# The first value load of a local-attention and gated-MLP kernel, issued right behind the up-projection weights

## The chip, the cores and the metric

The kernel runs on one core of a Trainium2 chip. The metric is device time in microseconds, the median of several executions. Three executions of the kernel before gave 264.83, 264.84 and 265.99 us, a median of 264.84. One further execution was profiled; all durations below come from it.

## The reference

The input x has 2048 tokens of width 640, in bf16. It is layer-normalised once, and two branches read the result:

```python
xn = _layernorm(x)                       # no gain, no bias
# branch A: 32 heads of width 20, window of 8 taps, 2 tokens apart, looking back
q, k, v = split(xn @ wqkv)
logits = einsum("bhsd,bhswd->bhsw", q, k[idx]) * 20 ** -0.5   # idx = pos - 2*w
logits = where(idx >= 0, logits, -1e9)
o = einsum("bhsw,bhswd->bhsd", softmax(logits), v[idx])
A = o @ wo
# branch B: bilinear gated MLP, hidden width 1536
B = ((xn @ w_gate) * (xn @ w_up)) @ w_down
out = x + A + B
```

Each token thus attends to itself and to the tokens 2, 4, ... 14 places before it, head by head.

## The kernel before, in words

**Tiles and chunks.** The 2048 tokens are 16 tiles of 128 (index t). Four tiles form a chunk of 512 (index c, 0 to 3). For each chunk, TensorE (PE) transposes or SyncE's DMA transposes the normalised tiles to `xnT` (lines 345 and 339), computes q and k (line 405) and, tile by tile, v (line 438). ScalarE (ACT) copies the results out of PSUM. v goes to a scratch tensor `vD` in DRAM (line 459, issued by GpSimd, POOL) with 14 rows of zeros in front, because the attention needs each row of v at eight shifts.

**Logits of a chunk.** VectorE (DVE) multiplies q by k at the eight shifts (line 476, `PW[8c]` to `PW[8c+7]`). Two products share one buffer called `pw`. PE adds them up per head in two groups of 40 matmuls (line 490, `LL[2c]`, `LL[2c+1]`), ACT copies the sums to `L` (line 503), and two DMA transposes on SyncE's queue (line 511, `SS[2c]`, `SS[2c+1]`) turn them to `LT`. These two are the chunk's logit transposes. DVE and ACT make the softmax weights `a` out of `LT` (lines 522 to 544; the first DVE step needs both transposes).

**Values of a tile.** One DMA on SyncE's queue (line 554, step `V8[t]`) gathers eight shifted copies of a tile's rows from `vD` to a buffer `v8`, 1280 KB. DVE multiplies it by the weights (line 579), folds the eight copies (lines 588, 592, 594) to `o`, and a DMA transpose (line 601, `OE[t]`) makes `oT`. The `v8` buffers and the `pw` buffers share one ring of five (`tag="pv"`, `bufs=5`): in chunk 0 the four `pw` buffers come first, `v8` of tile 0 takes the fifth, and `v8` of tile 1 takes over the first `pw` buffer, once `LL[0]` has read it.

**Gate, up, down.** PE computes gate and up for a chunk in 24 groups of five matmuls (line 621), ACT copies them (line 626), DVE multiplies the pair to `hT` (line 637, steps `HT[c, f]`, f from 0 to 11). Then, tile by tile, PE sums the down projection and the output projection in one PSUM tile (lines 662 and 665), DVE adds x (line 672) and a DMA stores the rows. The down projection of a chunk's first tile starts with `hT` 0 to 9.

**The order of the work.** A planner (`Plan.order`) simulates the engines with costs written in the code, and picks on each engine, among the steps that are ready, the one with the earliest latest start. The order that it finds is the order in which the instructions are emitted, and each engine runs its own in that order. What an instruction waits for at run time is only its data: who wrote what it reads, and who still reads what it overwrites. The `after=[...]` arguments, the costs and `floor` (an earliest planned end) act in the planner alone. For a DMA with `kb` set the planner also keeps one line of transfers per issuing engine, at 340 KB a microsecond, behind a start of 2 us.

**SyncE's queue around the change.** In the order of issue: w_gate (`wg`), x of tiles 9 to 12, w_up (`wu`, step `WL["u"]`), then chunk 0's two logit transposes, then `V8[0]`, `V8[1]`, w_down (`wd`), `V8[2]`, the transpose of o of tile 0 (`OE[0]`), four loads of `wo` (line 230), `V8[3]`. The list variable `SPLAST[0]` carries this chain in the planner. For `V8[0]` the planner's conditions are: behind `SPLAST[0]`, behind `PW[6]`, and the first stores of `vD` landed.

Of the kernel before, what the change touches and what calls it, by code (L numbers as in the profile page):

```python
# [31 lines left out]
class Plan:  # L32
# [8 lines left out]
    def add(self, eng, cost, fn, deps=(), occ=None, after=(), kb=0):  # L41
        s = Step(eng, cost, fn, deps, occ, after)
        s.kb = kb
        s.idx = len(self.steps)
        self.steps.append(s)
        return s
# [51 lines left out]
def kernel(  # L98
# [58 lines left out]
    def new(key, shape, dtype, tag, bufs, pool=None):  # L157
        t = (pool or sb).tile(shape, dtype, name=tag, tag=tag, bufs=bufs)
        T[key] = t
        return t  # L160
# [305 lines left out]
    PW, LL, LE, SS, DD, AA, O16, OE, V8, DT = {}, {}, {}, {}, {}, {}, {}, {}, {}, {}  # L466

    def prodlog(c):
        for g in range(2):
            for j in range(4):  # L470
                i = 4 * g + j

                def mul(i=i):
                    if i % 2 == 0:
                        new(("pw", c, i // 2), [P, 2, KT, CS], BF, "pv", 5)
                    nc.vector.tensor_tensor(T["pw", c, i // 2][:, i % 2, :, :], T["q", c][:],  # L476
                                            T["k", c][:, :, DIL * i : DIL * i + CS], ALU.mult)

                m = 8 * c + i
                w = [LL.get(2 * c - 1), O16.get(4 * c - 4), O16.get(4 * c - 3), O16.get(4 * c - 2)][i // 2]  # L480
                PW[m] = add("DVE", 1.48, mul, [*Q[c], *Kk[c], w], occ=1.395, after=[PW.get(m - 1) if i else V8.get(4 * c - 1)])
        LASTPW[c] = PW[m]
        for g in range(2):
            n = 2 * c + g

            def lg(g=g):
                l = new(("lps", c, g), [P, 512], F32, "pl", 2, psum)
                for i in range(KT):
                    for j in range(4):
                        nc.tensor.matmul(l[H * j : H * (j + 1), :], lhsT=Ek[:, i, :], rhs=T["pw", c, 2 * g + j // 2][:, j % 2, i, :],  # L490
                                         start=(i == 0), stop=(i == KT - 1), tile_position=(0, H * j),
                                         skip_group_check=True)

            LL[n] = add("PE", 1.25, lg, [PW[m], LL.get(n - 1), LE.get(n - 2), LE.get(n - 1 - g), CE], occ=1.12)
            LL[n].urgent = True
            LL[n].margin = 0.9

            def ev(g=g):
                L = new(("L", c, g), [P, CS], BF, "L", 2)
                if c == 0:  # L500
                    ps = T["lps", c, g]
                    nc.vector.tensor_tensor(ps[:, 0:HALO], ps[:, 0:HALO], negm[:, g, :], ALU.add)
                nc.scalar.copy(L[:], T["lps", c, g][:])

            LE[n] = add("ACT", 0.585, ev, [LL[n], SS.get(n - 2), CM], occ=0.5)

            def tr(g=g):
                if g == 0:
                    new(("LT", c), [P, CH, W, H], BF, "LT", 1)
                out = T["LT", c][:].rearrange("p t (g w) h -> p t g (w h)", g=2)[:, :, g, :]  # L510
                nc.sync.dma_start_transpose(out=out, in_=T["L", c, g][:])

            early = [SPLAST[0]] if c == 0 else []
            SS[n] = SPLAST[0] = add("SP", 3.5, tr, [LE[n], DD.get(2 * c - 1), DD.get(2 * c - 2)], occ=1.25, after=early, kb=160)

    def softmax(c, hf):
        n = 2 * c + hf

        def mx():
            L4 = T["LT", c][:, 2 * hf : 2 * hf + 2, :, :]  # L520
            m = sb.tile([P, 2, 4, H], BF, name="m", tag="m", bufs=1)
            nc.vector.tensor_tensor(m[:], L4[:, :, 0:4, :], L4[:, :, 4:8, :], ALU.max)
            nc.vector.tensor_tensor(m[:, :, 0:2, :], m[:, :, 0:2, :], m[:, :, 2:4, :], ALU.max)
            nc.vector.tensor_tensor(m[:, :, 0:1, :], m[:, :, 0:1, :], m[:, :, 1:2, :], ALU.max)
            d = new(("d", n), [P, 2, W, H], F32, "d", 2)
            nc.vector.tensor_tensor(d[:], L4, m[:, :, 0:1, :].to_broadcast([P, 2, W, H]), ALU.subtract)

        DD[n] = add("DVE", 1.52, mx, [SS[2 * c], SS[2 * c + 1], AA.get(n - 2)], occ=1.43)

        def ex():  # L530
            nc.scalar.activation(T["d", n][:], T["d", n][:], ACT.Exp, scale=scale)

        e = add("ACT", 0.635, ex, [DD[n]], occ=0.54)
        e.margin = 0.8

        def nrm():
            d = T["d", n]
            s = sb.tile([P, 2, 4, H], F32, name="s", tag="s", bufs=1)
            nc.vector.tensor_tensor(s[:], d[:, :, 0:4, :], d[:, :, 4:8, :], ALU.add)
            nc.vector.tensor_tensor(s[:, :, 0:2, :], s[:, :, 0:2, :], s[:, :, 2:4, :], ALU.add)  # L540
            nc.vector.tensor_tensor(s[:, :, 0:1, :], s[:, :, 0:1, :], s[:, :, 1:2, :], ALU.add)
            nc.vector.reciprocal(s[:, :, 0, :], s[:, :, 0, :])
            a = new(("a", n), [P, 2, W, H], BF, "a", 2)
            nc.vector.tensor_tensor(a[:], d[:], s[:, :, 0:1, :].to_broadcast([P, 2, W, H]), ALU.mult)

        AA[n] = add("DVE", 2.33, nrm, [e, O16.get(2 * n - 3)], occ=2.24)

    def load_v8(t):
        def fn():
            v = new(("v8", t), [P, W, D], BF, "pv", 5)  # L550
            r0 = t * P
            src = vD[r0 : r0 + P, :]
            src = bass.AP(tensor=src.tensor, offset=src.offset, ap=[[D, P], [DIL * D, W], [1, D]])
            nc.sync.dma_start(out=v[:], in_=src)
        order = [SPLAST[0]] if t < CH - 1 else [SS[2 * (t // CH) + 1]] if t % CH in (1, 2) else []
        c, u = divmod(t, CH)
        order.append(V8[t - 1] if u else PW[8 * c + 6])
        if t == 3:
            order.append(WL["o"])
        w = LL[2 * c + (u - 1) // 2] if u else O16.get(t - 1)  # L560
        V8[t] = add("SP", 6.0, fn, [VS[t], VS.get(t - 1), w, CZ], occ=0.5, after=order, kb=1280)
        if t < 3:
            SPLAST[0] = V8[t]
            V8[t].floor = (43.5, 0, 0)[t]

    def load_down():
        WL["d"] = SPLAST[0] = add("SP", 8, wload(wd, B_w_down), after=[SPLAST[0]], occ=0.5, kb=1920)
# [4 lines left out]
    def av(t):  # L572
        n, u = divmod(t, 2)
        if t > 2:
            load_v8(t)

        def mul():
            v = T["v8", t]
            nc.vector.tensor_tensor(  # L579
                v[:].rearrange("p w (j h) -> p w j h", j=Dh, h=H),  # L580
                v[:].rearrange("p w (j h) -> p w j h", j=Dh, h=H),
                T["a", n][:, u, :, None, :].to_broadcast([P, W, Dh, H]),
                ALU.mult,
            )

        def tree():
            v = T["v8", t]
            nc.vector.tensor_tensor(v[:, 0:4, :], v[:, 0:4, :], v[:, 4:8, :], ALU.add)  # L588

        def tree2():  # L590
            v = T["v8", t]
            nc.vector.tensor_tensor(v[:, 0:2, :], v[:, 0:2, :], v[:, 2:4, :], ALU.add)  # L592
            o = new(("o", t), [P, D], BF, "o", 2)
            nc.vector.tensor_tensor(o[:], v[:, 0, :], v[:, 1, :], ALU.add)

        a = add("DVE", 2.82, mul, [AA[n], V8[t]], occ=2.735)
        b = add("DVE", 1.485, tree, [a], occ=1.4)

        def tr():
            o = new(("oT", t), [P, KT, P], BF, "oT", 4)  # L600
            nc.sync.dma_start_transpose(out=o[:], in_=T["o", t][:])

        O16[t] = add("DVE", 1.35, tree2, [b, OE.get(t - 2)], occ=1.26)
        OE[t] = add("SP", 2.8, tr, [O16[t], DT.get(t - 4)], occ=1.3, kb=200, after=[V8[2]])
        if t == 0:
            SPLAST[0] = OE[0]
            load_out()
# [151 lines left out]
    def attention(c):  # L759
        if c == 0:  # L760
            SPLAST[0] = WL["u"]
        prodlog(c)
        if c == 0:
            load_v8(0)
            load_v8(1)
            load_down()
            load_v8(2)
        for hf in range(2):
            softmax(c, hf)
        for q in range(CH):  # L770
            av(c * CH + q)
# [47 lines left out]
```

## Time and profile before

| what | value |
|---|---|
| profiled execution: its time, and its span in the trace | 264.88 us, 263.2 us |
| PE busy, share of the span | 258.5 us, 98% |
| DVE busy | 214.7 us, 82% |
| ACT busy | 106.0 us, 40% |
| the sixteen value loads (1280 KB each), median time from issue to landing | 10.0 us |
| w_up, issue to landing | 12.2 us |
| w_down, issue to landing | 17.7 us |
| chunk 0's logit transposes, each | 2.4 and 2.5 us |

The granted TensorE clock was at full speed in all 40 slices of the span. In the lines below, the first two numbers of a timeline line are its start in the span and its length, and a bracket at the end holds the idle time of that engine just before, with what ended it. A time "to landing" runs from the issue of a DMA to its completion. In lists of waits the three numbers are the sum, how many times, and the longest. SPq is SyncE's own instruction queue, from which its DMAs are issued.

### The profile page before, as it was taken

The page shows a single profiled execution, that of the slowest core. Times are in us where ns is not written, and L with a number is a line of the kernel's source. Part 1 is how long each engine was busy: PE and PEld are TensorE (multiplying, and loading weights), DVE is VectorE, ACT ScalarE, POOL GpSimd, SP SyncE. Part 2 cuts the span into 40 slices and gives each one's busy share as a digit, 9 for nine tenths or more (in the row PEclk, how much of TensorE's full clock was granted, in tenths as well). Part 3 has the DMA queues.
Part 4 walks back from the last instruction along what each step waited for, and adds up shares of the span by engine and source line. Part 5 has one row for each costly group of instructions (what it writes and reads, how often), then busy time and mean ns, then how long its engine had stood idle before and what let it go on. Part 6 is the DMA issues. An engine that isn't in the chain of part 4 may idle for free.

```text
span 263.2 us, 4101 instructions
## 1 busy us (share of the span) xinstructions
PE 258.5 (98%) x1574; PEld 140.9 (54%) x1574; DVE 214.7 (82%) x337; ACT 106.0 (40%) x197; POOL 39.3 (15%) x84
## 2 busy tenths in 40 slices
PE   7999999999999999999999999999999999999995
PEld 2645455444677446444477554644456764445763
DVE  5775997799899999999999189999992999993221
ACT  2755557555200347455510155655541105554000
POOL 4651036000021121400001000420000004000000
PEclk9999999999999999999999999999999999999999
DMA  7998927999989149931167299451903985111001
GB/s 220 334 198 270 399 106 190 381 362 253 287 188 278 50 99 369 310 112 29 25 124 251 66 305 322 99 149 25 199 28 70 364 296 134 28 25 25 27 25 50
DMA packets 50707, 46.55 MB, mean 177 GB/s; under 512 B 24786, under 2 KB 47840, under 8 KB 50688
## 3 DMA queue, kind: packets, MB, share of 16 engines
q1 hardware_dynamic: 46704, 37.10, 50.1%
q0 software_dynamic: 2384, 8.05, 8.9%
q10 hardware_dynamic: 1600, 1.15, 1.4%
q8 instruction: 12, 0.20, 0.3%
q14 instruction: 7, 0.06, 0.1%
HBM read 35.39 MB, written 5.26 MB: 154 GB/s over the span
## 4 chain that ended last, share of the span: by engine, by line
PE 78%; DVE 11%; DMA 7%; SPq 1%; issue 0%; ACT 0%; DVEq 0%
PE ps L621 30%; PE ps L662 15%; PE ps L405 15%; DMA pv<-vD 7%; PE ps L438 7%; PE ps L665 6%; DVE pv L476 4%; DVE pv L579 3%; PE pl L490 3%; PE ps L242 2%; DVE xr L672 1%; DVE pv L588 1%; SPq L230 1%; DVE pv L592 1%; PE ps L345 0%
## 5 line engine op out<-in xcount | busy, mean ns | idle before, releaser
L621 PE MATMUL ps<-xnT,wg 128*128 128x512 bf16 x240 | 59.6, 379 | 0.0
L621 PE MATMUL ps<-xnT,wu 128*128 128x512 bf16 x240 | 59.6, 379 | 0.0
L662 PE MATMUL ps<-wd,hT 128*128 128x320 bf16 (+2 forms) x384 | 57.4, 299 | 0.0
L476 DVE TENSOR_TENSOR pv<-q,k 128x2560 bf16<-128x2560 bf16 x32 | 46.5, 1484 | 3.0 <-ACT k L412 3.0
L579 DVE TENSOR_TENSOR pv<-pv,a 128x5120 bf16<-128x5120 bf16 x16 | 45.1, 2820 | 3.0 <-DMA pv<-vD 2.9
L662 PEld LDWEIGHTS <-hT 128*128 128x128 bf16 x384 | 37.0, 98 | 16.5 <-issue 0.8
L626 ACT CAST gs<-ps 128x512 bf16<-128x512 f32 x48 | 28.2, 587 | 32.2 <-PE ps L621 32.2
L621 PEld LDWEIGHTS <-wu 128*128 128x128 bf16 x240 | 23.5, 98 | 28.3
L621 PEld LDWEIGHTS <-wg 128*128 128x128 bf16 x240 | 23.5, 98 | 27.7
L626 ACT CAST us<-ps 128x512 bf16<-128x512 f32 x48 | 28.2, 587 | 22.4 <-PE ps L621 22.0
L672 DVE TENSOR_TENSOR xr<-ps,xr 128x320 bf16<-128x320 f32 (+2 forms) x32 | 15.0, 486 | 24.5 <-PE ps L665 16.1
L665 PE MATMUL ps<-wo,oT 128*128 128x320 bf16 (+2 forms) x160 | 27.0, 299 | 0.0
L696 POOL DMA_DIRECT2D out_dram<-xr x14 | 7.6, 542 | 125.8 <-DVE xr L672 119.2
L588 DVE TENSOR_TENSOR pv<-pv 128x2560 bf16<-128x2560 bf16 x16 | 23.8, 1485 | 0.1
L438 PE MATMUL ps<-wv,xnT 128*128 128x320 bf16 x160 | 23.3, 300 | 0.4 <-ACT xnT L351 0.4
L412 ACT CAST q<-ps 128x512 bf16<-128x512 f32 x20 | 11.7, 585 | 27.8 <-PE ps L405 27.8
L637 DVE TENSOR_TENSOR hT<-gs,us 128x512 bf16<-128x512 bf16 x48 | 19.5, 419 | 4.0 <-ACT us L626 4.0
L405 PE MATMUL ps<-xnT,wq 128*128 128x512 bf16 x100 | 22.4, 379 | 0.0
L405 PE MATMUL ps<-xnT,wk 128*128 128x512 bf16 x100 | 22.2, 379 | 0.0
L438 PEld LDWEIGHTS <-xnT 128*128 128x128 bf16 x160 | 15.3, 98 | 7.5 <-ACT xnT L351 0.6
L665 PEld LDWEIGHTS <-oT 128*128 128x128 bf16 x160 | 15.5, 98 | 6.3
L444 ACT CAST v_t<-ps 128x320 bf16<-128x320 f32 x32 | 13.3, 429 | 7.4 <-PE ps L438 4.1
(54 smaller groups left out, 178.7 us busy)
## 6 DMA issues: line engine op xcount, KB each, us to landing
pv<-vD SPq DMA_DIRECT2D x16, 1280.0 KB, 10.0
vD<-v_t POOLq DMA_DIRECT2D x16, 160.0 KB, 4.5
xr<-in_A_x_dram POOLq DMA_DIRECT2D x16, 160.0 KB, 3.7
out_dram<-xr POOLq DMA_DIRECT2D x14, 160.0 KB, 3.5
wg<-in_B_w_gate_dram SPq DMA_DIRECT2D x1, 1920.0 KB, 8.1
wu<-in_B_w_up_dram SPq DMA_DIRECT2D x1, 1920.0 KB, 12.2
wd<-in_B_w_down_dram SPq DMA_DIRECT2D x1, 1920.0 KB, 17.7
x<-in_A_x_dram SPq DMA_DIRECT2D x11, 160.0 KB, 4.9
```

The source lines that it names most:

```text
L405: nc.tensor.matmul(T[key][:, 0:n], lhsT=(wk if r else wq)[:, i, j * P : (j + 1) * P], rhs=T["xnT", c][:, i, lo : lo + n], start=(i == 0), ...
L438: nc.tensor.matmul(T["psv", t, n][:, 0:NS], lhsT=T["xnT", c][:, i, q * P : (q + 1) * P], rhs=wv[:, i, n * NS : (n + 1) * NS], start=(i == ...
L444: nc.scalar.copy(T["v_t", t][:].rearrange("p (j h) -> p j h", j=Dh, h=H)[:, :, n * H // 2 : (n + 1) * H // 2], T["psv", t, n][:, 0:NS].rea ...
L476: nc.vector.tensor_tensor(T["pw", c, i // 2][:, i % 2, :, :], T["q", c][:], T["k", c][:, :, DIL * i : DIL * i + CS], ALU.mult)
L579: nc.vector.tensor_tensor(v[:].rearrange("p w (j h) -> p w j h", j=Dh, h=H), v[:].rearrange("p w (j h) -> p w j h", j=Dh, h=H), T["a", n][ ...
L588: nc.vector.tensor_tensor(v[:, 0:4, :], v[:, 0:4, :], v[:, 4:8, :], ALU.add)
L621: nc.tensor.matmul(ps[:], lhsT=(wu if r else wg)[:, i, f * P : (f + 1) * P], rhs=T["xnT", c][:, i, :], start=(i == 0), stop=(i == KT - 1))
L626: nc.scalar.copy(s[:], T[key][:])
L637: nc.vector.tensor_tensor(h[:], T["gs", c, f][:], T["us", c, f][:], ALU.mult)
L662: nc.tensor.matmul(ps, lhsT=T["hT", c, f][:, q * P : (q + 1) * P], rhs=wd[:, f, sl], start=(f == 0), stop=(f == FT - 1 and not wo_part))
L665: nc.tensor.matmul(ps, lhsT=T["oT", t][:, g, :], rhs=wo[:, g, sl], start=False, stop=(g == KT - 1 and f1 == FT))
L672: nc.vector.tensor_tensor(T["xr", t][:, sl], T["psD", t, n][:, 0:w], T["xr", t][:, sl], ALU.add)
```

## The change

`load_v8(0)`, which builds the step `V8[0]`, is called inside `prodlog(0)`, behind the eight products and in front of the two logit groups and their transposes; before, it was called after `prodlog(0)` had returned. `SPLAST[0]` is then still `WL["u"]`, so that the planner puts `V8[0]` right behind w_up on SyncE's queue, and the two logit transposes behind `V8[0]`. The second, third and fourth value loads and w_down keep their places. The planned earliest end of `V8[0]` goes from 43.5 to 40.0.

```diff
@@ prodlog(c), line 482
         LASTPW[c] = PW[m]
+        if c == 0:
+            load_v8(0)
         for g in range(2):
             n = 2 * c + g
@@ load_v8(t), line 561
         V8[t] = add("SP", 6.0, fn, [VS[t], VS.get(t - 1), w, CZ], occ=0.5, after=order, kb=1280)
         if t < 3:
             SPLAST[0] = V8[t]
-            V8[t].floor = (43.5, 0, 0)[t]
+            V8[t].floor = (40.0, 0, 0)[t]
@@ attention(c), line 762
         prodlog(c)
         if c == 0:
-            load_v8(0)
             load_v8(1)
             load_down()
             load_v8(2)
```

## The prediction

> **What bounds the kernel now.** I read the page's engine table first, then TensorE's waits, which say how much a better order can give at all; then VectorE's waits, which show what the first value load costs; then SyncE's timeline and the DMA landings, which show what the load will meet in its new place.
>
> ```profile
> PE 258.5 (98%) x1574; PEld 140.9 (54%) x1574; DVE 214.7 (82%) x337; ACT 106.0 (40%) x197; POOL 39.3 (15%) x84
> PE ps L242 <- DVE wv L192: 1.3, 1, 1.3
> PE ps L438 <- ACT xnT L351: 0.4, 1, 0.4
> PE pl L490 <- DVE pv L476: 0.3, 1, 0.3
> 93.05 1.24 PE L490 MATMUL pl<-pv,Ek 128*32 128x512 bf16 x17 [0.32 <-DVE pv L476]
> 68.38 1.52 PE L662 MATMUL ps<-wd,hT 128*128 128x320 bf16 x10
> ```
>
> PE is busy for 258.5 of 263.2 us. Its list of waits has three entries, 1.27, 0.36 and 0.32 us; with the 2.77 us between its last matmul (260.42, the chain of waits) and the end of the span they are the whole rest. The first two lie before 7 us and the last is the final addition and store. So only the 0.32 us at 93.05 can be touched: there PE has done chunk 1's first logit group and three matmuls of the second, and waits for the last product on DVE.
>
> ```profile
> 42.10 0.29 DVE L522 TENSOR_TENSOR m<-LT 128x256 bf16<-128x256 bf16 x1 [0.62 <-DMA LT<-L]
> 49.03 2.83 DVE L579 TENSOR_TENSOR pv<-pv,a 128x5120 bf16<-128x5120 bf16 x1 [1.33 <-DMA pv<-vD]
> 67.49 0.42 DVE L637 TENSOR_TENSOR hT<-gs,us 128x512 bf16<-128x512 bf16 x1
> 72.86 2.83 DVE L579 TENSOR_TENSOR pv<-pv,a 128x5120 bf16<-128x5120 bf16 x1 [1.61 <-DMA pv<-vD]
> ```
>
> DVE idles 1.33 us for tile 0's values, 1.61 us for tile 3's, and 0.62 us for the logit transposes. PE never stopped for the first of them. The third line is `HT[0, 9]`, the last input that PE needs for the down projection at 68.38: done at 67.91, it leaves PE 0.47 us.
>
> ```profile
> 20.12 0.58 SPq L172 DMA_DIRECT2D wg<-in_B_w_gate_dram  x1
> 20.80 2.22 SPq L166 DMA_DIRECT2D x<-in_A_x_dram  x4
> 23.06 0.45 SPq L172 DMA_DIRECT2D wu<-in_B_w_up_dram  x1
> 38.34 2.51 SPq L511 DMA_TRANSPOSE LT<-L  x2
> 40.96 1.15 SPq L554 DMA_DIRECT2D pv<-vD  x2
> 42.16 2.54 SPq L172 DMA_DIRECT2D wd<-in_B_w_down_dram  x1
> 44.87 7.86 SPq L554 DMA_DIRECT2D pv<-vD  x1
> ...
> x<-in_A_x_dram SPq DMA_DIRECT2D x4, 160.0 KB, 7.9
> ...
> 34.00:35.00 1.00, 1.00 (x7) 0.54 (x6) 1.00 (x3) 0.51 (x2) 0.00 (x0) 1.00 0.23 89
> 36.00:37.00 1.00, 1.00 (x21) 0.45 (x22) 1.00 (x4) 0.48 (x2) 0.05 (x1) 1.00 0.00 0
> ```
>
> SyncE issues nothing from 23.51 to 38.34. In the two stretches the last columns are clock, share of the DMA engines, and GB/s: they are full until about 34.25, when w_up's data ends, and then empty until about 38. The four x loads in the middle line, issued behind w_gate, took 7.9 us to land (the page's median is 4.9), about when w_gate was through (20.12 + 8.1 = 28.2): the queue serves its transfers in order.
>
> **The change, part by part.** *Removed:* the issue of the load between the logit transposes and `V8[1]`, half of the 1.15 us for two: `V8[1]` is issued about 0.57 us earlier, and so are w_down and `V8[2]`.
>
> *Added in front:* the same issue behind w_up. At run time it waits neither for `PW[6]` nor for the planned end; these order the plan alone. Its rows of `vD` come from the zero rows and from tile 0's store, issued by POOL at 9.65 (4.5 us to landing by the page, so 14.2), and its buffer is the ring's unused fifth. So I take its issue at 23.51, 0.58 us long. Were SyncE held up there for want of room, as `V8[2]` was for 7.86 us, the cover is the empty 14.8 us until 38.34.
>
> *When it lands.* In order behind w_up, its 1311 KB (1.311 million bytes) start at 34.25; at 412 GB/s, the best 1 us stretch under w_up, that is 3.2 us, and 1.0 us more from last data to landing, as w_up shows (34.25 to 35.26): 38.5. From the other side: the value loads at 137.5, 184.7 and 79.9, with little beside them, took 6.6, 7.4 and 7.3 us from issue to landing, and the one at 40.96 took 8.0; started only at w_up's landing, that is 41.9 to 43.3. The x loads queued behind w_gate paid no start of their own, so I take the near end, with some margin for 1280-byte rows: 39. w_up itself is in front and keeps its 35.3; even if both shared and it landed at 39, PE reads it first at 43.56.
>
> *The moved-past work.* The two logit transposes now stand behind this load. A landing at 39 has its last data at 38.0, so that nothing is left at 38.34; a landing at 40 would leave 0.7 us. I take a delay of 0.2. From the other end, a landing at 43.3 and then the second transpose's 1.2 us of issue give 44.5 in place of 42.1, so 2.4 us. Behind them wait DVE's softmax (42.10), ACT's exponentials, and on SyncE `V8[1]`. No POOL transfer is moved; the store at 36.95 shares the engines with the load's tail, and its rows are read by no value load before tile 4's.
>
> The rule that speaks against the change is a page's. The Trainium skill, "DMA: Bandwidth & Descriptors", section "Queues, rings and completion order", says that on each DMA engine a ring's descriptors are consumed in ring order. By that rule the transposes wait for everything left of the load; if the ring mixed them, w_up would land late instead and the transposes would not wait. The x loads above agree with the rule, and by it the second rival below exists at all; the sum comes out alike by both, 264.5.
>
> *The first multiply* then starts when DVE is free, 49.03 - 1.33 = 47.70, or 0.2 later: DVE gains 1.1 to 1.3 us. Next it needs `V8[1]` at about 54.1. That load now has the first one's place in the queue, which landed it at 48.96. `V8[2]` landed at 64.7 with the multiply at 64.76; with 1311 KB less in front at 362 GB/s (the 52 to 56 us stretch) it lands 3.6 us earlier, 61.1, against a need at 63.4. `V8[3]` was 1.61 us late; what is ahead of it on SyncE (the transpose of o, held 2.99 us at issue, and the four `wo` loads) also gets free some 3 us earlier, so most of that wait should go too. DVE's gain until 75 us is 1.1 at least, 2.9 at most.
>
> *The planner.* Every step behind might be reordered. I followed its rule by hand: `V8[0]` is now planned at 32.84 (behind `PW[6]`), to end at the floor of 40.0; the second transpose's planned end stays 41.40, bound by its own start. The multiplies behind `V8[1]` to `V8[3]` become ready sooner, but when DVE is free at those points it has a step with an earlier latest start, as before. So no order on PE, DVE, ACT or POOL should change, cost nothing.
>
> *Where the gain reaches the end.* The last product that PE waited for at 93.05 comes 1.1 us or more earlier, so the wait goes: -0.32. Behind it PE has no wait to lose, and gains none as long as DVE leads: its final logit group of chunk 3 at 197.15 comes after products done at 196.6, 0.5 us of room.
>
> **Sum.** Load off DVE's path: -1.33 to -2.94 on DVE, of which 0.32 on PE. 264.88 (263.2 of span and 1.7 around it) - 0.32 = 264.56; the profiled execution lies 0.04 above the median of 264.84, so 264.5.
>
> **Rivals.** *First, the wait stays.* DVE's lead is eaten again before 93 us, by `V8[3]` still landing near 72.8 and by evictions that wait for PE between 79 and 92; PE keeps 0.32 us: 264.8. For it: `V8[3]` leads or trails by tenths of a microsecond, and eight additions are laced into the products. Against it: the last down projection that they wait for is done at 86.85, and a lead of 0.32 us is enough.
>
> *Second, the transposes come late: slower.* The load lands late and delays both by d. DVE has 1.33 us to lose at 47.70, and `HT[0, 9]` another 0.47; from d = 1.8 on PE stalls at 68.38, one for one. At the bound d = 2.4 that is +0.6 and, as the late PE then finds the products done, -0.3: 265.1. With V8[0] still draining when the transposes are issued, they could also be held at issue as the transpose of o was (2.99 instead of 1.2 us): d up to 4.2, +2.4 - 0.3: 266.9. Over 0.5% it needs d above 3.4. For it: the queue serves in order. Against it: the DMA engines stood empty from 34.3 to 38.
>
> *Third, a much larger gain,* over 0.5%, needs 1.3 us off PE; the waits hold 0.32 past the start. I see no way but a faster execution as a whole.
>
> **How the numbers follow.** Half a per cent, 1.3 us (about what a measurement of this kernel can tell from no change), bounds "same": 263.5 to 266.2. Forecast 0.68 (264.2 to 264.7), the wait stays 0.16 (264.7 to 265.1), transposes late with the end below 266.2 0.06, above it 0.06, larger gain 0.02, something slower that I do not see 0.02. Faster 0.02, same 0.90, slower 0.08. The range, 264.1 to 265.5, leaves out the last three and part of the mild late case.
>
> **What would show it.** Right: SyncE issues the load near 23.5, it lands at 38 to 40; the first softmax step stays at 42.1 to 42.4; the multiply starts near 47.7 with no bracket; PE's list of waits loses the 0.3 us entry at L490 and gains none. Wrong: a PE wait for `hT` at 68, a longer issue of the transposes at 38.34, or an order on PE or DVE that differs.

## The result and the profile after

The changed kernel took 264.19 us (median of 18 executions, 264.01 to 265.08) against 265.16 us for the kernel before, measured beside it (18 executions, 264.43 to 266.86). The ratio is 0.9968, with a 95% interval of 0.9958 to 0.9979: by the ratio 0.85 us less, between 0.56 and 1.11 us (the two medians differ by 0.97). The prediction was 264.5 us, in a range of 264.1 to 265.5. Sign and range held, the range narrowly; the gain is over twice the 0.32 us of its sum.

The profiled execution of the changed kernel took 264.72 us, in the upper part of its 18. It lost some 0.5 us at the very start, before the change has any effect (TensorE's first q group of chunk 1 starts at 87.37 and not at 86.85, and the list of waits has 0.4 us for `wq`), so that its total is no measure of the change. Its stretches are. Lines 483 to 763 of the kernel before stand two lines further down here; in the edited kernels of the experiments line numbers shift by a few more.

First the engine table's line for TensorE, then its whole list of waits:

```profile
PE 258.2 (98%) x1574; PEld 140.4 (53%) x1574; DVE 214.6 (82%) x337; ACT 106.1 (40%) x197; POOL 39.4 (15%) x84
PE ps L242 <- DVE wv L192: 1.3, 1, 1.3
PE ps L405 <- DMA wq<-in_A_wqkv_dram: 0.4, 1, 0.4
PE ps L438 <- ACT xnT L351: 0.4, 1, 0.4
```

The wait at the logit matmuls is gone, and no new one stands behind 13 us. VectorE's timeline of the changed kernel, the same four places as before:

```profile
42.88 0.29 DVE L524 TENSOR_TENSOR m<-LT 128x256 bf16<-128x256 bf16 x1 [0.88 <-DMA LT<-L]
48.41 2.82 DVE L581 TENSOR_TENSOR pv<-pv,a 128x5120 bf16<-128x5120 bf16 x1
66.86 0.42 DVE L639 TENSOR_TENSOR hT<-gs,us 128x512 bf16<-128x512 bf16 x1
70.53 2.82 DVE L581 TENSOR_TENSOR pv<-pv,a 128x5120 bf16<-128x5120 bf16 x1
```

Both brackets of the value multiplies are gone, tile 0's (1.33 us) and tile 3's (1.61 us). With the 0.52 us of the start taken off, the first multiply begins at 47.89 and the fourth at 70.01: VectorE is 1.14 us ahead at the one and 2.85 us at the other. The softmax begins 0.26 us later than before, by the transposes.

SyncE's timeline and the landing of the first value load:

```profile
24.47 0.45 SPq L172 DMA_DIRECT2D wu<-in_B_w_up_dram  x1
25.02 1.38 SPq L556 DMA_DIRECT2D pv<-vD  x1
38.86 2.71 SPq L513 DMA_TRANSPOSE LT<-L  x2
41.75 0.44 SPq L556 DMA_DIRECT2D pv<-vD  x1
...
pv<-vD SPq DMA_DIRECT2D x1, 1280.0 KB, 14.9
...
38.00:39.00 1.00, 1.00 (x21) 0.36 (x14) 0.97 (x6) 0.59 (x1) 0.98 (x3) 1.00 1.18 397
39.00:40.00 1.00, 1.00 (x8) 0.70 (x8) 1.00 (x4) 0.62 (x2) 0.80 (x2) 1.00 0.39 138
```

The load goes out right behind w_up and lands at 25.02 + 14.9 = 39.9. In the two stretches the DMA engines are full until 39 and busy for 0.39 of the next microsecond, so they are nearly done with the load when the transposes are issued, at 38.86.

Where TensorE wins 0.69 us is seen in its timeline around chunk 1's logit groups. The kernel before, with VectorE's last product of the chunk as the last line (the line at 93.05 is shown in the prediction):

```profile
86.85 4.48 PE L405 MATMUL ps<-xnT,wq 128*128 128x512 bf16 x20
91.26 1.48 PE L490 MATMUL pl<-pv,Ek 128*32 128x512 bf16 x23
...
95.31 5.56 PE L405 MATMUL ps<-xnT,wk 128*128 128x512 bf16 x25
...
91.52 1.48 DVE L476 TENSOR_TENSOR pv<-q,k 128x2560 bf16<-128x2560 bf16 x1
```

The changed kernel:

```profile
87.37 4.48 PE L405 MATMUL ps<-xnT,wq 128*128 128x512 bf16 x20
91.78 2.34 PE L492 MATMUL pl<-pv,Ek 128*32 128x512 bf16 x40
94.05 1.25 PE L405 MATMUL ps<-xnT,wq 128*128 128x512 bf16 x5
95.14 5.56 PE L405 MATMUL ps<-xnT,wk 128*128 128x512 bf16 x25
...
89.18 1.48 DVE L476 TENSOR_TENSOR pv<-q,k 128x2560 bf16<-128x2560 bf16 x1
```

The last product is done at 93.00 before and at 90.66 after, 6.15 and 3.29 us behind the start of TensorE's q group: 2.86 us sooner, which is VectorE's gain at the fourth multiply.

From the first q group to the first k group TensorE does the same work in 95.31 - 86.85 = 8.46 us before and in 95.14 - 87.37 = 7.77 us after. I call this the q-to-k stretch; it is the measure in the experiments below. Its 0.69 us lies inside the measured gain's interval.

### The profile page after: what moved, and what is told of

Read it like the earlier page. It is cut to its first block, busy times and chain, and to the rows that moved or that the text cites. A ratio compares the mean times of both kernels' runs of the same rounds, so it can differ in the third digit from the quotient of the medians.

```text
span 263.0 us, 4102 instructions
## 1 busy us (share of the span) xinstructions
PE 258.2 (98%) x1574; PEld 140.4 (53%) x1574; DVE 214.6 (82%) x337; ACT 106.1 (40%) x197; POOL 39.4 (15%) x84
## 4 chain that ended last, share of the span: by engine, by line
PE 94%; DMA 3%; DVE 1%; issue 0%
PE ps L623 39%; PE ps L664 20%; PE ps L405 17%; PE ps L667 8%; PE ps L438 7%; PE pl L492 3%; DMA wq<-in_A_wqkv_dram 3%; DMA x<-in_A_x_dram 1%; DVE st L251 1%; DVE xr L674 0%; DVE mv L257 0%; DVE ve L259 0%; DVE x L270 0%
## 5 line engine op out<-in xcount | busy, mean ns | idle before, releaser
L251 DVE BATCH_NORM_STATS2 st<-x 128x6 f32<-128x320 bf16 x32 | 13.9, 481 | 4.4 <-DMA x<-in_A_x_dram 4.4
```

Source lines behind the costliest of these rows:

```text
L251: nc.vector.bn_stats(T["st", t][:, g, :], T["x", t][:, g * NS : (g + 1) * NS])
```

## The experiments

Theory one: the gain is TensorE's stall in that stretch, which goes because VectorE, freed from two waits for value loads, has the last product of chunk 1 ready in time. The rival: the gain comes from the load's new place in another way (less crowding on the DMA engines later, or another engine), and the lead of VectorE is beside the point.

**The kernel before, once more.**

> The kernel before, unchanged, profiled once more. Theory one: the whole gain (265.16 to 264.19 in medians) is TensorE's wait in front of chunk 1's second logit group, and it was 0.32 us in the first profile only by chance; in another execution the wait is as long as VectorE is late, so that this profile's time less its wait at line 490 comes to 264.0 to 264.6 us, as the first did (264.88 - 0.32 = 264.56). Rival: the wait is always near 0.3 us and the rest of the gain, some 0.6 us, comes from elsewhere; then time less wait is up to 266.

It took 264.80 us, with the same stall (0.32 us shown, a q-to-k stretch of 8.46 us). Time less wait is 264.48, inside theory one's bounds, but the guess behind it fell: the wait was not small by chance. The profile shows 0.32 us, and the stretch costs 0.69.

**The same added work on VectorE in both kernels.** The edit, in each:

```diff
-                    nc.vector.tensor_tensor(T["pw", c, i // 2][:, i % 2, :, :], ...)
+                    for _ in range(2 if c == 1 and i == 0 else 1):
+                        nc.vector.tensor_tensor(T["pw", c, i // 2][:, i % 2, :, :], ...)
```

> The kernel before, with the first product of chunk 1 computed twice (1.40 us more on VectorE, same output). Theory one: VectorE is already the one that TensorE waits for at line 490, so that all 1.4 us comes out at the end: 266.2 to 266.7 us, ratio 1.005 to 1.006, a wait of 1.7 us at line 490. Rival (VectorE has room there): ratio 1.000 to 1.002.

> The changed kernel, with the same first product of chunk 1 computed twice (1.40 us more on VectorE). Theory one: the change gave VectorE a lead of 2.5 us there (the last product ends at 90.66, TensorE comes to the second logit group at 92.98 and needs it at its fourth matmul), so the 1.4 us are hidden: 264.2 us, ratio 0.996 to 0.998 to the kernel before, no wait at line 492. Rival (the gain does not come from VectorE's lead, which is used up): 265.3 to 265.7 us.

In the kernel before, 1.40 us more on VectorE made it 266.59 us against 264.74 without, ratio 1.0065 (1.0046 to 1.0084); the q-to-k stretch went from 8.46 to 9.98 us. In the changed kernel they cost nothing: 264.13 us, ratio 0.9977 (0.9966 to 0.9988) to the kernel before, and a stretch of 7.78 us. TensorE's wait in the first of the two:

```profile
PE pl L491 <- DVE pv L477: 1.4, 1, 1.4
```

That is 1.4 and not the 1.7 us expected: a part of the wait does not show as idle, as the 23 matmuls ahead of it are shown as 1.89 us long, where it was 1.48.

So the changed kernel has room on VectorE at just the place where the kernel before has none. With three more products, 4.2 us, in the changed kernel:

> The changed kernel, with the first product of chunk 1 computed four times (4.2 us more on VectorE, same output). Theory one: VectorE's lead at the second logit group is 2.4 us (the last product ends at 90.66, the fourth matmul that needs it would be issued near 93.1), so 1.8 us come out, and 0.2 to 0.4 us more for the split group of matmuls: 266.0 to 266.6 us. Rival (the lead is 1.3 us only, what the first load's wait was): 267.2 us and more.

Its profile, of an execution of 266.21 us, has a q-to-k stretch of 96.63 - 86.63 = 10.00 us, 2.23 more than without, so that some 2 us of the 4.2 were hidden: theory one's size. But the profiled execution was the fastest of four, which went from 266.21 to 268.60. Their median, 267.4, is outside the expected 266.0 to 266.6 and by the number alone it is the rival's. One more profile of the same kernel was taken for that:

> The same kernel as with the first product of chunk 1 computed four times, profiled once more, since its times went from 266.2 to 268.6 us. If VectorE's own chain between 42 and 93 us varies from run to run, this profile's time is 264.2 us less 7.77 plus the time that TensorE takes from its first q group to its first k group of chunk 1, whatever that is (10.00 us in the profile of 266.21). If something later varies, time and that stretch do not go together.

It took 266.52 us with a stretch of 96.95 - 86.96 = 9.99 us (264.2 - 7.77 + 9.99 = 266.4). Both profiled executions agree with the reckoning, and so with theory one's lead. What made the others up to 2 us longer, no profile has caught, and it stays open.

**The same lead without the load.** Two ways were tried to remove the stall in the kernel before with the load left where it was. The first moves one step of TensorE:

```diff
-    for s in plan.order():
+    steps = plan.order()
+    at = steps.index(LL[2])
+    nxt = next(k for k in range(steps.index(LL[3]) + 1, len(steps)) if steps[k].eng == "PE")
+    steps.insert(at, steps.pop(nxt))
+    for s in steps:
         s.fn()
```

> The kernel before, with one step of TensorE moved: the fifth q group of chunk 1 (five matmuls, 1.08 us) is done ahead of chunk 1's two logit groups, not behind them. Nothing else moves, the value load keeps its old place. Theory one (the gain is the wait at line 490): TensorE reaches the second logit group 1.08 us later with the same work done, the wait of 0.32 us or more goes, and the time falls as by the change itself, ratio 0.995 to 0.999 to the kernel before. Rival (the gain comes from the load's new place, through the DMA queue or another engine): no gain, ratio 0.999 to 1.001.

No gain: 264.84 us, ratio 0.9999 (0.9990 to 1.0009). Read alone, that is the rival's result. Its list of waits shows a new stall:

```profile
PE ps L621 <- ACT v_t L444: 0.6, 1, 0.6
```

The q-to-k stretch did become 7.77 us (86.75 to 94.52). But the logit transposes went out 1.0 us later (94.20 and not 93.21), and the three value loads behind them 0.6 us later (96.86). By the chain of waits the store of a v tile, issued at 103.94, then took until 109.90; ScalarE's copy of the last v tile waited for it until 110.00 (108.68 in the kernel before), and TensorE for that copy until 110.47. The store had gone out at 103.24 in the kernel before. One stall was exchanged for another of about the same size. What made the store late and slow is not shown: in the last run below the transposes go out later still (95.55), and this stall does not come. The second way leaves TensorE's order alone and moves two additions of VectorE behind the last product:

```diff
+    steps = plan.order()
+    for s in OB[3].deps:
+        steps.remove(s)
+    at = steps.index(PW[15]) + 1
+    steps[at:at] = OB[3].deps
```

> The kernel before, with two 0.40 us additions of VectorE (line 672, tile 3) done behind chunk 1's last product and not in front of it. The value load keeps its old place, no other instruction moves. Theory one: the last product ends 0.8 us sooner, TensorE's stall at line 490 goes, and with it 0.69 us, which is what TensorE took longer from its first q group of chunk 1 to its first k group in the kernel before (86.85 to 95.31) than in the changed one (87.37 to 95.14): ratio 0.9974, interval within 0.996 to 0.999. Rival (the gain needs the load's new place): ratio 0.999 to 1.001.

264.34 us, ratio 0.998 (0.9969 to 0.9990): a gain of 0.5 us (0.3 to 0.8) without touching the load. TensorE's timeline of this run:

```profile
87.22 4.48 PE L405 MATMUL ps<-xnT,wq 128*128 128x512 bf16 x20
91.63 2.60 PE L490 MATMUL pl<-pv,Ek 128*32 128x512 bf16 x40
94.16 1.25 PE L405 MATMUL ps<-xnT,wq 128*128 128x512 bf16 x5
95.25 2.11 PE L405 MATMUL ps<-xnT,wk 128*128 128x512 bf16 x9
```

The 40 matmuls take 2.60 us and not 2.34: the last product ended at 92.93, just as TensorE got there, so that 0.26 us of the stall is left. Against TensorE's q group the product came 0.44 us sooner and not the 0.8 expected; VectorE waited 3.3 us in sum for value loads here (2.9 in the kernel before). The stretch is 8.03 us, 0.43 less than before, and the time fell by that within its interval. The gain thus needs no new place of the load, only a last product that is early enough. This is the run that settles theory one.

One count holds the runs together. From the start of TensorE's first k group of chunk 1 (95.31 in the kernel before) to the end of the measured time of the profiled execution there are 169.56 to 169.60 us in ten profiles: two of the kernel before, one of the changed kernel, four with added products, this one, and the two with a delayed load below. So whatever these edits did to the time, they did ahead of that point. The run with the moved q group has 170.40, its later stall.

**How late may the transposes be?** The prediction's second rival was tested by making the load late in its new place: a VectorE write into its buffer, which the load must wait for.

```diff
             v = new(("v8", t), [P, W, D], BF, "pv", 5)
+            if t == 0:
+                nc.vector.memset(v[0:1, 0, 0:2], 0.0)
```

> The changed kernel, with the first value load still in front of the logit transposes on SyncE's queue, but made to wait for a small VectorE write into its buffer, placed where the first transpose's input is being copied (near 38 us); it is then issued near 38.2 us and not at 25. If the queue serves in order, its data takes the engines from 39.7 to 43.3 and the transposes land near 45.7 and not 42.9, d = 2.8 to 3.3 us; VectorE has 1.6 us of room at hT 9 (done 67.28, needed 68.89), so TensorE stalls 1.2 to 1.7 us at 68.9: 265.4 to 266.0 us. Rival (transposes pass a load ahead of them in the queue): they land by 43.5, no stall: 264.0 to 264.3 us.

In this run and the next the load is also planned behind the first logit copy. The write did not stand where the expectation said: it came behind the seventh product, and the load went out at 33.16. Two lines of its SyncE and VectorE timelines:

```profile
33.16 0.38 SPq L559 DMA_DIRECT2D pv<-vD  x1
...
43.41 0.29 DVE L525 TENSOR_TENSOR m<-LT 128x256 bf16<-128x256 bf16 x1 [2.05 <-DMA LT<-L]
```

The softmax starts 1.3 us later than in the kernel before, and that costs nothing: 264.20 us, ratio 0.9971 (0.9959 to 0.9983). So the load need not go right behind w_up; eight microseconds later does as well. The first multiply starts at 48.94 here, hardly sooner than the 49.03 of the kernel before, and only the fourth is clearly ahead (71.06 against 72.86). Of VectorE's two waits it is thus tile 3's, the last one ahead of chunk 1's products, whose loss carries the gain here; the first one, from which I had started, need not go. In the next run the planner counts no time and no transfer for the load, and the write stands where it was meant to:

> The changed kernel, with the first value load still in front of the logit transposes on SyncE's queue, and waiting for a small VectorE write into its buffer that now stands behind line 251's statistics of tile 12 and so runs near 38.2 us (in the run before this, the write stood behind the seventh product, and the load was issued at 33.16). Issued at 38.3, the load lands 6.6 to 7.4 us later, as the value loads with little beside them did in the kernel before: 44.9 to 45.7. If the transposes wait behind its data, they land at 45.5 to 46.5 and not at 42.0, d near 4; hT 9 is then done near 70.6 against a need at 68.3, TensorE stalls 2 to 2.5 us there, and the time is 266.2 to 266.8 us. Rival (transposes pass the load): they land by 43.5 and the time is 264.2 us, with VectorE waiting for the load instead.

266.16 us, ratio 1.0043 (1.0027 to 1.006). From its SyncE, VectorE and TensorE timelines, with the landings of the load and the first transpose in the middle:

```profile
38.51 0.38 SPq L559 DMA_DIRECT2D pv<-vD  x1
38.93 2.70 SPq L514 DMA_TRANSPOSE LT<-L  x2
...
pv<-vD SPq DMA_DIRECT2D x1, 1280.0 KB, 6.7
LT<-L SPq DMA_TRANSPOSE x1, 6.8
...
46.60 0.29 DVE L525 TENSOR_TENSOR m<-LT 128x256 bf16<-128x256 bf16 x1 [5.07 <-DMA LT<-L]
...
71.05 0.31 PE L669 MATMUL ps<-wd,hT 128*128 128x320 bf16 x1 [1.21 <-DVE hT L644]
```

The load lands at 38.51 + 6.7 = 45.2, and the first transpose, 2.4 us when nothing is ahead, needs 6.8 and lands at 45.7. The DMA packets of this run between 39.5 and 43.7 us, and between 43.7 and 44.75:

```profile
DMA packets 879, 1.13 MB, mean 268 GB/s; under 512 B 0, under 2 KB 879, under 8 KB 879
DMA packets 623, 0.30 MB, mean 285 GB/s; under 512 B 478, under 2 KB 623, under 8 KB 623
```

Of the 879 packets in the first stretch none is under 512 bytes, of the 623 in the second 478 are. The small ones are the transposes' (in the kernel before, with only the two transposes on SyncE's queue from 38.34 to 40.9 us, 581 of 591 packets are under 512 bytes). The first transpose was issued at 38.93, and none of its packets moves until the load's are nearly through. The transposes wait here for a plain load ahead of them on the same queue. The Trainium skill, "DMA: Bandwidth & Descriptors", section "Queues, rings and completion order", says that on each DMA engine a ring's descriptors are consumed in ring order; this trace agrees, 6.8 against 2.4 us. The softmax is 4.5 us late, `hT` 9 comes late, and TensorE stalls at the tenth matmul of the down projection. The same order on SyncE's queue is a gain of 0.3% or a loss of 0.4%, by when the load goes out.

**The planned end alone.** Last, the second part of the diff was undone: the load in its new place, its planned earliest end left at 43.5.

```diff
-            V8[t].floor = (40.0, 0, 0)[t]
+            V8[t].floor = (43.5, 0, 0)[t]
```

> The changed kernel, with only the planned earliest end of the load left at 43.5. Worked through the planner, the two transposes are then planned to end at 43.97 and 44.44 and not at 40.47 and 41.40, VectorE's softmax is planned 3 us later, two products hT of the gate stand in front of it and other steps change places, TensorE's logit groups of chunk 1 two q and k groups later among them. If that order is as good as the other: 264.2 us. If the later transposes of chunk 1 cost as the run with the q group moved did (a stall of 0.6 us at 110 us): 264.7 to 265.2 us. I expect the second.

264.24 us, ratio 0.9976 (0.9965 to 0.9986). I had expected the stall at 110 us to come back, and it did not; TensorE's list has only three waits, all of the start. So the gain does not hang on the planned end. But this run does not show what the load's new place is worth, because the orders differ. VectorE takes two products of the gate ahead and gains little: its first multiply starts at 50.68, its fourth at 72.72, and the last product is done at 92.86 (49.03, 72.86 and 93.00 in the kernel before). TensorE does chunk 1's logit groups behind one q and one k group more, at 93.60, and so finds the products done. The stall is gone because TensorE comes later, and one cannot read off the planner's order alone whether it costs.

## Why the prediction was right, and where its sizes were off

*Issue and landing.* Right. The load went out right behind w_up, without waiting for its planned start. SyncE was held 1.38 us and not 0.58 for it, hidden as the prediction said it would be. It landed at 39.9, against 39 predicted; w_up itself had been issued 1.4 us later in this execution. (The best stretch under w_up had 415 GB/s, at 29 us, and not 412; the sum does not feel it.)

*The transposes behind it.* Right: the softmax is 0.26 us late, against 0.2. The sign of being wrong that the prediction named, a longer issue of the transposes, was there in small: 2.71 us and not 2.51.

*The gain on VectorE.* Right in kind, at the upper end: 1.1 us at the first multiply and 2.85 us at the fourth, against bounds of 1.1 to 2.9. Tile 3's wait went entirely, as `wo` (issued at 56.18 and not at 58.59) and the load behind it came sooner. That mattered: had tile 3's load still landed at 72.8, the lead of the first multiply would have been lost there.

*The planner.* Right: apart from SyncE's queue every engine issues its instructions in the same order.

*The sum.* The mechanism was right and the term was mis-sized: "The last product that PE waited for at 93.05 comes 1.1 us or more earlier, so the wait goes: -0.32." The stall costs 0.69 us by the q-to-k stretch, in two profiles of the kernel before alike. The profile's idle time is not what a stall costs here. The 40 matmuls of the two groups run unsplit in 2.27 us, 57 ns each. A q matmul, whose moving operand has 512 columns like theirs, takes 218 ns (five in 1.09 us, 94.05 to 95.14), nearly four times as long, as if four of the logit matmuls, each on 32 columns of the array, went side by side. The wait cut one such set of four, three before and one after; if the lone one takes the time of a whole set, that is some 0.2 us. Another 0.16 us is the tail of the last matmul before the wait, which the profile counts as busy (the five q matmuls at 94.05 are shown as 1.25 us long, and the next group starts 1.09 us after them; the 23 logit matmuls in 1.48 us are six times 0.218 and 0.17 more). 0.32 + 0.2 + 0.16 is an estimate of 0.68; no run separates its parts. The run with the moved additions lost 0.26 us with no idle shown at all. The Trainium skill, "Perfetto Trace Analysis", in its note ahead of the first section, warns that matmul busy time is a bad metric for how close a kernel is to its limit, as matmuls are pipelined; this trace agrees that busy time hides loss, 0.32 us of idle for 0.69 us of loss. With 0.69 the sum would have been 264.88 - 0.69 - 0.04 = 264.15, and 264.19 was measured. That 264.19 still lay inside the range was some luck: the 0.4 us that the range left below 264.5 were not there for this reason. The step "So only the 0.32 us at 93.05 can be touched" has the same error.

*The rivals.* The first (the wait stays) did not happen. The second was rightly kept unlikely: the engines were nearly done with the load when the transposes came. Its price was too high. The prediction gave VectorE 1.33 + 0.47 us, beyond which TensorE stalls one for one, and 0.3 us back because a late TensorE then finds the products done. A delay of 4.5 us should by that have cost 2.7 us at 68 us. It cost 1.4 us there: the wait ends at 71.05, and it sits at the tenth matmul of the down projection, which needs `hT` 9, and not at the first at 68.45, so that there were nine matmuls of 0.136 us, 1.2 us, of room more than I counted. And the 0.3 us did not come back: the 16 matmuls at 73.97 took 0.28 us longer than in the run before, and 0.26 us were lost at chunk 1's logit group (a stretch of 8.03 us). Together that is 1.9 us of the 2.0 by which 266.16 lies above the 264.20 us of the run before.

*The third rival, a much larger gain,* did not happen: no execution of any kernel here came out below 264.0 us.

## What to carry to other kernels

A load that waits for nothing new can be issued long before its first use, into a stretch in which the DMA engines stand empty; what must be checked is what stands behind it on its queue at the moment when its data is still moving. Where one engine is busy for 98% of the span, the whole worth of such a move is the stall it removes there, and the stall is best measured as the difference between two like stretches of work, not as the idle time that the profile prints. An experiment that removes the same stall in another way can fail for a reason of its own: look at where its time went before giving up the theory.

## What the runs showed that I had not expected

- A wait that the profile shows as 0.32 us cost TensorE 0.69 us. An estimate puts some 0.2 us of it to a cut set of four matmuls; that is not shown.
- The wait that the change was aimed at, VectorE's for the first value load, need not go for the gain: with the first multiply at its old time (48.94 against 49.03) the kernel still took 264.20 us; it is tile 3's multiply that came sooner there (71.06 against 72.86).
- A change of TensorE's order that removed this stall (0.69 us) was paid back in full 16 us later, by a copy on ScalarE that waited for a store's buffer (TensorE's wait 0.64 us at 110.47).
- The added work on VectorE in the changed kernel gave executions from 266.2 to 268.6 us, a spread that the two profiled ones (266.21 and 266.52) do not explain.
